# Loads of x in short pieces with six places, zeros moved behind the softmax, and a newly searched order

## The chip, the cores and the metric

The kernel runs on one core of one Trainium2 chip. The metric is the device time of one execution in microseconds (us); lower is better. Of several runs the median is given. A profile is one more execution, recorded by the hardware profiler; its span goes from the first to the last instruction of the program, and its own time lies a little over the span.

Five engines work side by side: TensorE (PE; its weight loads are shown as PEld), VectorE (DVE), ScalarE (ACT), GpSimd (POOL) and SyncE (SP). Each has its own stream of instructions, executed in order, and they wait for each other through semaphores. Data moves between HBM and the on-chip memory by DMA.

## The reference

Two layers follow each other. The first is a causal convolution of 7 taps, whose weights come from a softmax and differ by head (8 heads of 24 columns). The second mixes tokens; its matrix product over all tokens can be regrouped.

```python
# x: (8, 4224, 192), weight: (8, 7)
w = softmax(weight, axis=-1)
x_pad = concatenate([zeros((B, 6, D)), x], axis=1)
out[b, s, h*24+g] = sum_k w[h, k] * x_pad[b, s + k, h*24+g]

# y = out; w_q, w_k: (192, 64), w_out: (192, 192)
wq, wk = y @ w_q, y @ w_k
W_tok = scale * einsum('bsd,btd->bst', wq, wk)
mixed = einsum('bst,btd->bsd', W_tok, y)
return maximum(mixed, 0) @ w_out
```

## The kernel before

Everything on the chip is in bf16, except sums and the output. x of all 8 batches has room on the chip at once (`XW`), so no load of x ever waits for a buffer.

**Tiling.** A batch of 4224 tokens is cut into 35 chunks (`NCC`) of 122 tokens. A chunk is loaded as 128 rows, 6 of them from the chunk before, so that the convolution becomes one matrix product with a band matrix `BAND` for each head. Chunk 0 (122 rows and 6 rows of zeros) and chunk 34 (82 rows) have loads of their own. Chunks are worked on in groups (`groups_of`): four groups of up to 9 for batch 0, two groups (18 and 17) for each other batch.

**Loads.** `gen_load` makes the loads of one group: one DMA for all its full chunks, plus the small one at the batch's start or end. POOL issues them, converting f32 to bf16 on the way; they are all of POOL's work apart from the identity matrix (`ident`). All loads of a group count on one semaphore. The three weights come over SP, after the second group of batch 0 has landed.

**Start.** `WT_F` (the softmax input) is loaded by SP. DVE writes ones, several zeros and then, step by step, the softmax: `wmx` (L461), two subtractions (L467, L473), the sum, the reciprocal and the taps (L494); ACT does the exponential. PE spreads the taps over the diagonals (`spread`, L508) into two PSUM banks, and ACT and DVE copy one bank each into `BAND` (L527).

**Per batch**, for each group: `conv` on PE (four operations, each with two heads in halves: L391 and L392 through the helper `halves`) and its eviction to `Y` (L671, ACT or DVE). Then over chunks: the transposes `tr_lo` (L395, L396) and `tr_hi` (L726), evicted to `YTL` and `YTH` (L698, L733); the queries `wq` (L751, L755), evicted to `WQT`; the Gram matrix `gram` of Y (L787), summed in a bank of its own over the batch. From this a small matrix M is made (`turn`, `m`), and for each of five blocks of tokens `mix_lo` (L878) and `mix_hi` (L890) give the mixed tokens, evicted with relu to `RT` (L907, L908). `fin_hi` (L935) and `fin_lo` (L391, L392) multiply with `w_out`, the result is evicted to `OUT` (L970) and stored by SP (L978).

**Tile shapes of PE.** `mix_lo` and `fin_hi` use weights of 64 rows and 128 columns, everything else weights of 128 (or fewer) rows and 64 columns, in pairs. The planner counts a cost (`SWITCH`) where PE changes from one to the other.

**Order.** All operations are listed first, each with what it needs, a length and a due time. `Planner.plan` then puts them in an order, engine by engine, always the operation that can begin and whose due time is lowest. The due times are the numbers in `TURNS`, one for each operation, found beforehand by a search; `STAY` is added where PE would change the tile shape, `HOLD` is how long it may wait for an operation of the same shape. `op.lands` and `op.tail` tell the planner when a load is to be counted as landed. `Program.place` writes the streams and puts in a wait for each semaphore that an engine isn't yet known to have passed; a second and further wait is an instruction of its own (L269).

Of the kernel before, what the change touches and what calls it, by code (L numbers as in the profile page):

```python
# [13 lines left out]
    int(t) / 1000  # L14
    for t in """
-9360 -9860 -8870 -8880 -9260 -9760 -9760 -9160 -9060 -8960 -8910 -8910 -8860 -9360 -9310 -9360 -9360
-9300 -9290 -9280 -8360 -8260 -8210 -8360 -8160 -7960 -7910 -7860 -7360 -7260 -6960 -7260 -4360 -10360
-4260 -4160 -4060 -4040 -3360 -3260 -3160 -4360 -4360 -4360 -4360 -4360 -4360 -4360 -4360 -4360 -4360
-3360 -3340 -3260 -3240 -2360 -2340 -2260 -2240 -1360 -1340 -1260 -1240 -360 -340 -260 -240 640 660 740
760 1640 1660 1740 1760 2640 2660 2740 2760 -480 -5256 -3269 -5639 -2436 -6119 -4785 -6922 -2697 -6547  # L20
-2900 -8184 -3709 -11773 -2741 -3270 -6090 -11945 -3405 -6849 535 -5290 -3070 -5355 -2914 -5199 -4248
-3270 -5203 -8176 -5200 -3617 1049 7270 -1527 1452 -125 437 -1115 2575 669 4462 -4008 2241 -736 2188
-3392 2688 -366 4671 2314 4774 1510 -5859 -1080 1650 3655 -2805 -2225 2863 3712 -4982 -214 3624 -440
5811 168 -43 -4182 2328 1099 2977 4333 5544 2125 -4960 -5487 -5264 -3044 -1246 -5292 -632 -6217 -764
-74 -1078 1645 -1059 -604 310 -1847 1633 809 1261 1148 1774 613 1995 -221 2133 3240 -1868 3227 -220 725
-412 3895 1345 -3908 -437 2412 1145 -3912 1759 7529 -2401 -2511 -376 -45 -770 179 75 1157 1606 377 1178
2478 1419 2696 -2691 660 4785 4565 7183 -1945 323 1366 4118 -874 -955 202 -527 -342 -901 930 -907 356
2535 1985 1382 772 4127 1260 -1111 124 1160 1068 -949 2843 737 1947 1165 1141 1963 1865 1015 1391 1447
1702 -74 1049 2157 -573 -696 2171 3091 -3875 1621 1815 2057 1336 1560 3406 350 3930 1811 1631 806 1533
-2176 120 -160 307 697 392 -607 2158 1443 1095 4683 784 2578 2771 4703 2742 7357 3260 5899 3463 6217  # L30
3645 8560 -333 6048 2165 -3227 -299 4804 1442 -269 2464 1033 2330 -2282 2380 4417 716 -49 3007 5023
2635 1331 4441 4948 2995 6849 3538 5333 2785 2768 -3179 -2909 4430 6167 8185 2441 2170 3478 2909 2541
554 -2341 2444 1927 -821 1930 2471 1683 3865 3015 2812 1681 1913 2901 2236 -1040 2160 2775 2437 2022
2264 1982 2456 530 2945 -625 83 2391 2437 -247 4869 10274 3843 686 -2295 3278 468 -2877 2621 3234 3552
5619 5142 2314 3447 -712 2811 2566 3158 2537 2842 2785 -1373 2551 2194 3151 4852 2972 5013 3067 6779
3044 1235 3763 8267 3776 5123 4769 7025 4778 6514 4876 4862 2843 3189 4464 -186 3400 3287 1517 170 3082
4632 173 2822 4141 2345 4919 -1156 3870 4328 3579 2730 2456 3119 1411 4084 5177 4842 -327 4148 4784
2483 12403 11388 12726 1688 187 6372 10131 3246 4258 -1702 3458 4182 -118 2930 2729 1882 4669 8253 3861
3544 1615 3872 -172 2986 3160 3716 -1740 4531 9062 4005 3598 4951 3990 4363 2435 3391 -188 774 5121
6256 1049 3585 3961 4077 3890 4171 3621 2923 4666 7097 2748 2343 3820 2734 3811 2033 5780 3818 8021  # L40
2648 2954 4015 5571 3280 -1286 3326 1296 4205 -77 4486 1455 4875 3311 5075 4171 5445 4695 5467 3840
5547 6065 4545 4764 3889 874 4988 5384 3296 1407 5065 3706 4229 1167 4799 5495 -1008 2735 5015 4824
-216 1086 4797 3220 6247 4075 6903 8096 2585 2446 2397 3366 12419 11466 9645 4504 4002 2353 3004 4592
2447 1923 4855 3304 3544 3930 4268 4563 -31 1642 3776 4290 -862 3100 4826 6478 4160 4860 2445 3040 6705
3413 4148 6792 4180 4104 2785 4391 4686 4414 786 5937 2381 5714 4010 4678 4791 3602 4621 5486 -3702
4694 4691 4776 4745 8565 4811 2733 1579 4439 3726 3846 1552 3006 3416 5091 3731 3114 391 4950 -191 4947
1241 5561 6938 5922 7844 6076 5816 6857 5549 6431 8495 5919 4361 1180 965 5336 3713 5074 2853 2377 5685
3499 1703 6336 5580 6743 3976 5914 890 3735 -850 6119 5447 4947 4119 5702 6592 2952 2914 3851 5062
11027 10134 10283 4336 4832 2354 5585 5204 5235 5902 4279 5332 6811 4930 5452 70 7184 7777 5311 5310
3592 2752 3699 4914 5160 5093 886 6992 7265 5826 4610 2412 5386 6402 2677 5391 5863 3510 6078 4797 3048  # L50
3549 7308 4286 5112 2810 5621 5940 3872 3652 3847 6176 6516 2312 5811 4551 3444 5310 2800 3910 6703
2902 3118 6150 4601 5838 5604 6069 7926 5802 5058 6795 5408 6694 6497 7055 7466 7544 6117 8040 8562
2857 4878 6430 1709 6339 6247 4084 2149 3587 4651 7375 5911 5923 8233 4224 5104 7135 8548 7626 1422
6752 7520 5954 8811 9981 10001 3331 2861 1100 5523 5736 7942 8989 6855 6991 3418 3771 5267 6754 6792
5257 8583 2774 5930 5621 6098 8589 5981 7588 10163 5667 7262 8790 2009 6160 6573 7890 9275 9286 4367
8366 1994 4430 8376 2928 6391 6798 7671 9079 8471 6945 8447 929 3104 8245 1738 6621 7113 7765 8298
10610 7609 8976 2499 6811 5339 3124 4383 3701 4861 7650 5674 5118 6955 3022 7026 1967 7057 1554 7391
6867 7378 5794 8478 7540 10493 11198 10567 7886 9868 8667 7608 6132 7813 12143 8053 10500 4734 5726
10278 10809 6108 7660 6892 9279 8811 10480 9400 11789 6610 6051 11636 12987 12320 10573 10429 10064
11172 6766 7180 6653 8881 8940 8302 8163 3734 5115 8337 5917 10881 1732 6196 10991 548 6570 3947 6628  # L60
5684 11786 5374 8456 5972 5205 7358 2365 6800 7531 8553 12143 9541 7507 4239 2615 6653 8229 3661 7031
8556 8852 7269 9218 4711 5758 2449 5650 7927 7690 7261 10545 9140 8476 10487 4525 3241 2208 7451 8457
7788 6544 11624 6678 6638 3216 7890 3616 6282 3822 7930 5698 8782 6900 4062 5129 6641 6131 8120 8832
8094 4423 8160 8786 8210 8027 5877 5536 6062 1738 8351 8563 8713 4799 8391 5602 10941 9278 9705 9844
6685 7724 8581 9175 4769 3738 8621 7276 9572 10940 8347 11120 8993 5619 8811
# [38 lines left out]
class Planner:  # L104
# [6 lines left out]
    STAY = 0.865  # L111

    HOLD = 1
# [166 lines left out]
def bass_lightweight_conv__then__hypermixer_token_mlp_kernel(  # L280
# [43 lines left out]
    def semaphore(name):  # L324
        return es.enter_context(nc.semaphore(name))
# [48 lines left out]
    def bank(i, n=1):  # L374
        return PS[:, i * 512 : (i + n) * 512]
# [18 lines left out]
    def turn_halves(e, out, in_, identity):  # L394
# [34 lines left out]
        1250,  # L429
# [28 lines left out]
        200, needs=[ident], vt=-8.92)  # L458
# [44 lines left out]


    bands = []
    for q0, engine in ((0, "ACT"), (4, "DVE")):

        def spread(e, op, q0=q0):  # L508
            last = None
            for q in range(q0, q0 + 4):  # L510
                last = halves(
                    e,
                    bank(op.bank)[:, (q - q0) * 128 : (q - q0 + 1) * 128],
                    STEPT[0:112, 112 - 16 * q : 240 - 16 * q],
                    TAPS[0:112, :, :].rearrange("p i h -> p (i h)"),
                    start=q == q0,
                    stop=q == q0 + 3,
                    skip_group_check=True,
                )
            return last  # L520

        fill = add("PE", spread, 260, needs=[taps, stept], banks=1, vt=-7 + 0.1 * q0)

        def band(e, op, q0=q0, fill=fill):
            dst = BAND[:, :, 16 * q0 : 16 * q0 + 64]
            src = bank(fill.bank).rearrange("p (j h) -> p h j", h=H)
            return e.copy(dst, src) if op.engine == "ACT" else e.tensor_copy(dst, src)  # L527

        bands.append(add(engine, band, 550, drains=fill, vt=-6.9))
# [3 lines left out]
    at = [5000.0]  # L533

    def gen_load(b, gi):
        sem = semaphore(f"s_x{b}_{gi}")
# [4 lines left out]
        if cs[0] == 0:  # L541
            parts.append((XW[KC - 1 : 128, b, 0, :], bass.AP(x_t, base, [[D, CW], [1, D]])))
        n = len(full)
        parts.append(
            (
                XW[:, b, full[0] : full[0] + n, :],
                bass.AP(x_t, base + (CW * full[0] - KC + 1) * D, [[D, 128], [CW * D, n], [1, D]]),
            )
        )
# [9 lines left out]
        at[0] += len(cs) * 260.0  # L559
        load[b, gi] = []  # L560
        for k, part in enumerate(parts):
            first = (b, gi) == (0, 0) and part[0].shape[1] > 1 and len(part[0].shape) == 3
            op = add(
                "POOL",
                lambda e, op, part=part: e.dma_start(*part),  # L565
                900,
                needs=[zero_x] if cs[-1] == NCC - 1 else [],
                after=[] if first else [ident],
                dma=(f"x{b}_{gi}", sem, 16),
                vt=-10 if first else -4 + b + gi * 0.1 + 0.02 * k,  # L570
            )
            op.tail = 1500.0
            op.lands = at[0]
# [485 lines left out]
```

## Time and profile before

| what | us |
|---|---|
| median of 3 runs | 177.06 (177.01 to 177.64) |
| the profiled execution | 177.53 |
| its span | 175.7 |
| first `conv` matmul | 8.76 |
| second `conv` group of batch 0 | 11.62 |
| first `conv` of batch 1 | 23.53 |
| first `conv` of the last group | 133.97 |
| last store issued | 171.7 |

Mean granted clock of TensorE in this execution: 0.990.

Some landings of x, from issue to the moment when the whole load was there: the first load (8 chunks of batch 0) 1.30 to 6.46 us; the second group of batch 0 3.21 to 10.79; the last of batch 0 6.14 to 15.14; the 17 chunks of batch 1's first group 7.23 to 21.30; those of its second group 25.59 with the last; the first group of batch 2 30.25; the last load of all 52.46 to 106.0.

The page gives the DMA loads of the queues as a share of 16 engines' time. A share over 100% in a stretch means that one DMA engine had more than one packet under way.

```
q0 software_dynamic: 36128, 13.61, 65.1%      (x; POOL)
q1 hardware_dynamic: 12000, 26.31, 40.9%      (weights and out; SP)
q8 instruction: 25, 0.41, 0.9%
```

The columns are packets, MB and share. In lines of waits the columns are: who waited, for whom, us in total, times, longest. In a timeline they are: start, length, engine, line, operation, tiles and shapes, and in brackets the idle time of the engine before it. "issue" stands for a wait that no semaphore in the profile explains.

### The profile page before, as it was taken

The numbers are of one execution on the slowest core, as the hardware profiler recorded it, in microseconds if no ns is written. First come the engines' busy times: TensorE is split into PE (matmuls) and PEld (weight loads), VectorE is DVE, ScalarE is ACT, GpSimd is POOL, SyncE is SP. The second block draws the span as 40 slices with busy tenths as digits, with TensorE's granted clock in tenths as the row PEclk, the third lists the DMA queues.
The fourth block names the chain that finished last, engine by engine and source line by source line (L and its number), as shares of the span: only waits on it lengthen the run. The fifth ranks groups of instructions, "written<-read, shape, count | busy, mean of one in ns | idle before, by whom it ended". The sixth has DMA issues, their size and how long they took to land.

```text
span 175.7 us, 7099 instructions
## 1 busy us (share of the span) xinstructions
PE 157.1 (89%) x3226; PEld 121.7 (69%) x3226; DVE 118.0 (67%) x216; ACT 123.5 (70%) x206; POOL 30.3 (17%) x39
## 2 busy tenths in 40 slices
PE   0289799888999999899989979999999999999990
PEld 0179666776787787668778766878767777877550
DVE  6556587765766677586787738689688675765740
ACT  3243677597787948668648747888888896698980
POOL 7999452524230000000000000000000000000000
PEclk9999999999999999999999999999999999999995
DMA  3999999999999999999999999067283045987787
GB/s 30 162 189 186 205 191 193 191 196 277 193 279 194 286 309 268 343 250 243 304 264 282 237 194 348 24 244 297 103 343 127 4 175 216 356 347 309 265 303 262
DMA packets 48157, 40.36 MB, mean 230 GB/s; under 512 B 37632, under 2 KB 40960, under 8 KB 48128
## 3 DMA queue, kind: packets, MB, share of 16 engines
q0 software_dynamic: 36128, 13.61, 65.1%
q1 hardware_dynamic: 12000, 26.31, 40.9%
q8 instruction: 25, 0.41, 0.9%
q14 instruction: 4, 0.03, 0.1%
HBM read 27.56 MB, written 25.95 MB: 305 GB/s over the span
## 4 chain that ended last, share of the span: by engine, by line
PE 88%; issue 4%; DVE 3%; ACT 2%
PE ps L391 25%; PE ps L787 14%; PE ps L935 8%; PE ps L392 7%; PE ps L395 6%; PE ps L726 6%; PE ps L878 5%; PE ps L751 4%; PE ps L890 4%; PE ps L755 4%; PE ps L396 3%; ACT rt L907 1%; ACT out_sb L970 1%; DVE band L527 0%; DVE xw L416 0%
## 5 line engine op out<-in xcount | busy, mean ns | idle before, releaser
L970 ACT COPY out_sb<-ps 128x768 f32<-128x768 f32 (+1 forms) x46 | 34.7, 768 | 15.1 <-PE ps L392 11.3
L671 ACT CAST y<-ps 122x816 bf16<-122x816 f32 (+3 forms) x46 | 35.7, 791 | 13.2 <-PE ps L392 12.8
L907 ACT ACTIVATE rt<-ps 128x1024 bf16<-128x1024 f32 (+3 forms) x44 | 34.1, 800 | 6.4 <-PE ps L878 4.5
L787 PE MATMUL ps<-y 122*64 122x192 bf16 (+4 forms) x840 | 33.8, 222 | 2.2 <-issue 2.2
L970 DVE COPY out_sb<-ps 128x768 f32<-128x768 f32 (+1 forms) x26 | 21.6, 840 | 19.7 <-PE ps L392 18.5
L392 PE MATMUL ps<-wol,rt 128*64 128x192 bf16 x264 | 33.9, 255 | 1.0 <-issue 1.0
L787 PEld LDWEIGHTS ps<-y 122*64 122x64 bf16 (+1 forms) x840 | 31.1, 112 | 4.9 <-issue 2.8
L565 POOL DMA_DIRECT2D xw<-in_x_dram x34 | 29.9, 893 | 22.3 <-issue 21.5
L391 PE MATMUL ps<-wol,rt 128*64 128x192 bf16 x264 | 33.7, 255 | 0.0
L391 PE MATMUL ps<-xw,band 128*64 128x432 bf16 (+3 forms) x144 | 31.8, 335 | 1.5 <-DVE band L527 0.9
L392 PE MATMUL ps<-xw,band 128*64 128x432 bf16 (+3 forms) x144 | 32.1, 337 | 1.1 <-issue 1.1
L391 PEld LDWEIGHTS ps<-wol,rt 128*64 128x64 bf16 x264 | 24.1, 138 | 8.1 <-issue 2.0
L908 DVE TENSOR_SCALAR rt<-ps 128x512 bf16<-128x512 f32 (+3 forms) x36 | 23.6, 674 | 8.2 <-PE ps L878 7.6
L671 DVE CAST y<-ps 122x864 bf16<-122x864 f32 (+3 forms) x26 | 23.6, 912 | 8.0 <-PE ps L392 7.5
L698 DVE COPY ytl<-ps 128x976 bf16<-128x976 bf16 (+1 forms) x40 | 23.0, 591 | 3.9 <-PE ps L396 3.3
L392 PEld LDWEIGHTS ps<-wol,rt 128*64 128x64 bf16 x264 | 24.1, 138 | 1.2 <-issue 1.2
L396 PE MATMUL ps<-ident,y 122*64 122x122 bf16 x280 | 21.1, 219 | 0.0
L395 PE MATMUL ps<-ident,y 122*64 122x122 bf16 x280 | 21.0, 219 | 0.0
L935 PE MATMUL ps<-woh,rt 64*128 64x192 bf16 x264 | 20.4, 250 | 0.2 <-ACT rt L907 0.2
L395 PEld LDWEIGHTS ps<-ident,y 122*64 122x64 bf16 x280 | 18.1, 112 | 2.0 <-issue 0.5
L726 PE MATMUL ps<-ident,y 122*64 122x122 bf16 (+1 forms) x344 | 17.1, 220 | 1.3 <-DVE y L671 0.7
L396 PEld LDWEIGHTS ps<-ident,y 122*64 122x64 bf16 x280 | 17.7, 112 | 0.0
(95 smaller groups left out, 218.8 us busy)
## 6 DMA issues: line engine op xcount, KB each, us to landing
out_dram<-out_sb SPq DMA_DIRECT2D x28, 768.0 KB, 5.1
xw<-in_x_dram POOLq DMA_DIRECT2D x7, 816.0 KB, 33.2
xw<-in_x_dram POOLq DMA_DIRECT2D x7, 768.0 KB, 33.7
out_dram<-out_sb SPq DMA_DIRECT2D x8, 384.0 KB, 3.3
xw<-in_x_dram POOLq DMA_DIRECT2D x2, 432.0 KB, 8.3
out_dram<-out_sb SPq DMA_DIRECT2D x8, 96.0 KB, 4.3
xw<-in_x_dram POOLq DMA_DIRECT2D x1, 384.0 KB, 5.2
xw<-in_x_dram POOLq DMA_DIRECT2D x8, 45.8 KB, 25.0
```

The source lines that it names most:

```text
L391: e.matmul(out[0:64], lhsT[:, 0:64], rhs, **k)
L392: return e.matmul(out[64:128], lhsT[:, 64:128], rhs, **k)
L395: e.transpose(out[0:64], in_[:, 0:64], identity)
L396: return e.transpose(out[64:128], in_[:, 64:128], identity)
L565: lambda e, op, part=part: e.dma_start(*part),
L671: return e.copy(dst, src) if op.engine == "ACT" else e.tensor_copy(dst, src)
L726: last = e.transpose(ps[64 * i : 64 * i + HI, o : o + w], Y[0:w, yb, c, LO:D], IDENT[0:w, 0:w])
L787: mm = e.matmul(bank(GB)[p : p + 64, o : o + z - r], Y[0:w, yb, c, r : r + 64], Y[0:w, yb, c, r:z], start=st, stop=end, skip_group_check=True,
L907: return e.activation(dst, src(), AF.Relu)
L908: return e.tensor_scalar(dst, src(), 0.0, None, op0=ALU.max)
L935: last = e.matmul(bank(op.bank + a)[:, o : o + D], RT[64 * a : 64 * a + HI, slot, 2, i:n:nt], WOH[64 * a : 64 * a + HI, :], start=i == q, ...
L970: return e.copy(dst, src) if op.engine == "ACT" else e.tensor_copy(dst, src)
```

## The change

**Loads.** For batches 1 to 7 the full chunks of a group are loaded in pieces of two chunks (one piece of three in the group of 17), so a batch has 18 loads instead of 4. There are six semaphores, taken in turn. From the seventh on, a load waits on POOL until the load six before it, which had the same semaphore, has landed. Batch 0 is loaded as before, but with a semaphore for each load. A group's first `conv` waits for all semaphores that its loads counted on. The planner gets other figures for loads (issue, `tail`, `lands`).

**Zeros.** The memsets of `WQT`, `WQH`, `YTH`, `WKT`, `WKB` and `MBD` on DVE come after `taps`, the last step of the softmax.

**Band.** It is spread into four PSUM banks instead of two, in pieces of 32 columns a head, which ACT and DVE copy in turn.

**Order.** `TURNS`, `STAY` and `HOLD` are new, and the planner's length of `ident`.

```diff
@@ TURNS, STAY, HOLD
-    int(t) / 1000
+    int(t) / 1e6
...
-    STAY = 0.865
-
-    HOLD = 1
+    STAY = 1.104146
+
+    HOLD = 2.100438
@@ ident, own: the planner's length and due time
-        1250,
+        700,
...
@@ zeros
+    for zero in (zero_w, zero_q, zero_yt, *zero_k, zero_m):
+        zero.after.append(taps)
@@ band
-    for q0, engine in ((0, "ACT"), (4, "DVE")):
+    for q0, engine in ((0, "ACT"), (2, "DVE"), (4, "ACT"), (6, "DVE")):
...
-            for q in range(q0, q0 + 4):
+            for q in range(q0, q0 + 2):
...
-            dst = BAND[:, :, 16 * q0 : 16 * q0 + 64]
-            src = bank(fill.bank).rearrange("p (j h) -> p h j", h=H)
+            dst = BAND[:, :, 16 * q0 : 16 * q0 + 32]
+            src = bank(fill.bank)[:, 0 : 32 * H].rearrange("p (j h) -> p h j", h=H)
@@ gen_load
-    at = [5000.0]
+    NLOAD = 6
+    S_LOAD = [semaphore(f"s_x{i}") for i in range(NLOAD)]
+    small_loads = []
+    LANDS = [6000.0, 9900.0, 12300.0, 13900.0]
...
-        n = len(full)
-        parts.append(
-            (
-                XW[:, b, full[0] : full[0] + n, :],
-                bass.AP(x_t, base + (CW * full[0] - KC + 1) * D, [[D, 128], [CW * D, n], [1, D]]),
+        pieces = len(full) // 2 if b else 1
+        for k in range(pieces):
+            some = full[len(full) * k // pieces : len(full) * (k + 1) // pieces]
+            parts.append(
+                (
+                    XW[:, b, some[0] : some[0] + len(some), :],
+                    bass.AP(x_t, base + (CW * some[0] - KC + 1) * D, [[D, 128], [CW * D, len(some)], [1, D]]),
+                )
             )
...
+            slot = len(small_loads) % NLOAD
+            gate = small_loads[-NLOAD:][:1] if b and len(small_loads) >= NLOAD else []
             op = add(
                 "POOL",
                 lambda e, op, part=part: e.dma_start(*part),
-                900,
-                needs=[zero_x] if cs[-1] == NCC - 1 else [],
-                after=[] if first else [ident],
-                dma=(f"x{b}_{gi}", sem, 16),
+                610 if b else 900,
+                needs=[*([zero_x] if cs[-1] == NCC - 1 else []), *gate],
+                after=small_loads[-1:] if b else [] if first else [ident],
+                dma=(f"x_{slot}", S_LOAD[slot], 16) if b else (f"x0_{gi}_{k}", semaphore(f"s_x0_{gi}_{k}"), 16),
...
-            op.tail = 1500.0
-            op.lands = at[0]
+            op.tail = 4200.0 if b else 1500.0
+            op.lands = 0.0 if b else LANDS[gi]
+            if b:
+                small_loads.append(op)
```

## The prediction, made before the result was known

> **What bounds the kernel now.** I read the first two parts of the page first, then sums by stretch of time, then TensorE's own waits, then the DMA view.
>
> ```profile
> PE 157.1 (89%) x3226; PEld 121.7 (69%) x3226; DVE 118.0 (67%) x216; ACT 123.5 (70%) x206; POOL 30.3 (17%) x39
> PE   0289799888999999899989979999999999999990
> DMA  3999999999999999999999999067283045987787
> ```
>
> TensorE (PE) sets the end. DVE and ACT have a third of their time free. PE's row has dents in its first 60%, none after that; DMA is full over the same 60%. The table by stretch (PE, PEld, DVE, ACT, POOL busy, clock, DMA share, GB/s) says the same in microseconds:
>
> ```profile
> 16.00:106.00 90.00, 84.59 (x1834) 66.99 (x1828) 62.58 (x108) 63.93 (x111) 15.49 (x18) 1.00 1.40 245
> 106.00:170.00 64.00, 63.80 (x1265) 47.15 (x1263) 46.00 (x79) 53.87 (x86) 0.00 (x0) 1.00 0.59 227
> ```
>
> From 16 to 106 us PE is idle for 5.41 us, from 106 to 170 us for 0.20. The granted clock is 1.00 in both. 106 us is when the last x has landed: its load was issued at 52.46 us and landed 53.5 later. What PE waits for (us in total, times, longest):
>
> ```profile
> PE ps L395 <- DVE step L435: 3.6, 1, 3.6
> PE ps L391 <- DVE taps L494: 2.9, 1, 2.9
> PE ps L787 <- issue: 2.2, 2, 1.3
> PE ps L392 <- issue: 2.1, 2, 1.1
> PE ps L391 <- DVE band L527: 0.9, 1, 0.9
> PE ps L726 <- DVE y L671: 0.7, 1, 0.7
> PE ps L391 <- issue: 0.6, 1, 0.6
> PE ps L726 <- issue: 0.5, 1, 0.5
> ```
>
> The waits for DVE all lie before 11.2 us: the softmax and the band matrix. The "issue" waits are the 5.41 us: 1.28 at 19.20 us, 0.08 at 26.86, 0.50 at 32.64, 1.07 at 39.08, 0.90 at 70.06, 0.59 at 89.60, 0.99 at 102.10. No semaphore explains them; one is in the middle of one `fin_lo`:
>
> ```profile
> 101.85 0.25 PE L391 MATMUL ps<-wol,rt 128*64 128x192 bf16 x1
> 103.09 0.30 PE L392 MATMUL ps<-wol,rt 128*64 128x192 bf16 x1 [0.99 <-issue]
> ```
>
> The DMA view of 100.7 to 102 us shows what went before it:
>
> ```profile
> q8 instruction: 1, 0.02, 4.6%
> ```
>
> Each of the six long waits has such a packet shortly before it: it starts at 18.01, 30.78, 37.69, 68.66, 87.76 and 100.72 us, takes 0.95, and PE goes on 1.35 to 1.5 us after its end. All 25 are 16 KB. So PE's instructions arrive by DMA, and PE runs dry when one is late. The packets before 101 us follow each other by 6.0 to 6.9 us (13 intervals), the first one with x nearly done by 3.8 (100.72, 104.50): x in the rings costs such a fetch up to some 2.5 us. After 106 us none is late enough to stall PE, though stores of out go on.
>
> **The change part by part**, against the profiled execution (span 175.7, time 177.53, so 1.8 outside the span; it is 0.47 over the median of 177.06).
>
> *Loads in pieces.* Batches 1 to 7 get 126 loads for 28, almost all of two chunks: 256 packets, 16 for each of 16 DMA engines, where a load of 17 chunks puts 136 on each. At most six stand in the rings; before, POOL put in what the rings would take (it waited seven times for "issue", 21.5 us). The trace has no fetch behind short loads, so bounds: nothing gained (0), or all seven stalls gone (-5.4). If a fetch comes 0.63 us earlier (a quarter of the 2.5), 0.65 + 0.44 + 0.27 + 0.36 = 1.7 us of stalls stay; at 1.25 us earlier 0.03. I take 1.4 us left, since loads that are held back also last longer and meet more fetches: **-4.0**.
>
> The Trainium skill (DMA: Bandwidth & Descriptors, "Queues, rings and completion order") says that each DMA engine goes round its queue rows and drains one packet, typically 9 to 17 descriptors and at most 64, before it changes rows. By that rule it does not matter how many loads are queued behind the first, and a limit of six alone gains nothing; only shorter packets would. The trace is on its side in one point: the stall at 19.20 us, with loads that took 14 us to land, is no shorter than that at 102.10 us, with loads that took 53.
>
> *The gate.* Each of these loads waits on POOL for the one six before it. Behind it on POOL are only later loads, and behind those the `conv` of their group. A load of 2 chunks should cost POOL 0.55 (the 122-row load) + 134/2054 of the way to 1.28 (17 chunks): 0.60 us. Round trip, by the nearest rows: 2.9 us (`wt_f`, 28 KB) at least, 5.2 (the first load, 8 chunks on empty rings) at most; over six, 0.48 to 0.87 us a piece, with POOL's 0.60 as the floor. Before, these 126 pieces' worth landed from 15.1 to 106.0 us: 0.72 each. What the new order can stand: I counted the matmuls ahead of each group's first `conv` in the built program, took when that many had begun in the trace, less the stalls until then, and set it against the old landing. Batch 1: matmul 273, 22.56 - 1.28 = 21.28 against 21.3, slack 0.0; its second half (408) 28.26 against 25.6, slack 2.7. Batch 2 (626) 38.55 against 30.25, 8.3; last group (2510) 128.3 against 106.0, 22.3. So only batch 1 is near its load. Bounds 0 to +1.5; I take **+0.5**.
>
> *Semaphores.* A group's first `conv` waits for six instead of one. In the built programs PE has 80 semaphore instructions for 48; the trace's take 51 ns each. 32 x 51 ns = 1.6 if all are exposed, 0 if matmuls of 408 columns cover them (they do in mid-stream, where PE shows no gap around one). I take **+0.3**.
>
> *Zeros behind the softmax; band in four.* The six memsets take 0.40 us (3.02 to 3.42, ahead of `step`) and 0.42 (4.28 to 4.70, ahead of `wmx`, whose weights landed at 3.75). `taps` ends 0.8 earlier, at 5.9. Then they run while DVE would wait for PE (1.16 us idle before L527), but end near 6.8, after the first fill. Two casts of 256 columns on each of DVE and ACT, at some 0.40 (0.69 and 0.58 for 512), end near 7.6: first `conv` at 7.75 instead of 8.76, -1.0. The x for it landed at 6.77. But `gram` now stands right behind the second `conv` group and waits for its eviction, as L726 waits 0.70 now, with nothing between: +0.7. Together **-0.3** (bounds -1.0 to +0.2).
>
> *Order.* The same 3226 matmuls. Tile shape changes between 64-row and 128-row weights 98 times for 106. Such a step (L935 to L391, 101.46 to 101.63) takes 0.17 us, a step inside `fin_lo` 0.08: 8 x 0.1 = **-0.8** (bounds -1.2 to 0; new waits for an eviction up to +1.5, which DVE and ACT at 70% make unlikely).
>
> Sum: -4.0 + 0.5 + 0.3 - 0.3 - 0.8 = -4.3. Span 171.4, time 172.8 set against the median.
>
> **Rivals.** (a) *Forecast, fetches come in time*: 172.8, 0.58. (b) *The fetch wait is fixed, stalls stay*: a fetch waits for what one engine already has in hand, six pieces or sixty. For it: the stalls do not grow with the backlog. Against: they end with the last x, and pieces put 16, not 136, packets on an engine at once. Then the sum is -0.3: 176.8, 0.15. (The rule of the Trainium skill above would give this, if it is the number of loads that matters.) (c) *Batch 1 comes late*: its slack is 0.0, and its seventh to ninth piece wait for a landing near 15.4 us. Two more microseconds at that `conv`: 174.8, 0.11. (d) *The gate throttles x*: if a round trip stays above 6 x 0.90 = 5.4 us, the last group misses 128.3 us ((128.3 - 15.1) / 126 = 0.90). At 5.7 us (0.95 a piece) it lands at 134.8, 6.5 late, against the 4.3 gained: 179.3. For it: landings of 5.2 us alone, up to 33 behind others, and the stores share the engines from 36 us. Against: 0.72 with full rings. 0.13. (e) *New waits for evictions* of 3 us: 175.8, 0.03.
>
> **How the numbers follow.** The time is (a)'s. Its own range, all stalls gone and the best order to few gone, is 170.3 to 174.9. (b), (c) and (e) carry it to 177.3; (d) is left out above. Within 0.5% (0.9 us, about what a measurement of this kernel can tell from no change) lies most of (b) beside the first half microsecond of (d). Faster: (a), (c), (e) and a third of (b), 0.77. Same 0.08. Slower, the rest of (d) and a little of (b), 0.15.
>
> **What would show it.** In the new profile: PE's "issue" waits before the last x lands fall from 5.4 to about 1.4 us, and 16 KB instruction packets keep their number; if they stay with shorter loads, (b). No wait of the first `conv` of a group for x beyond batch 1; if there are, (d), and POOL's landings are over 5.4 us. First `conv` near 7.75 us, and a new gap near 12 to 14 us. Wrong altogether, if PE waits for evictions in mid-stream, where it now has none.

## The result, and the profile after

The changed kernel takes 187.22 us (median of 4, 186.91 to 188.49), the kernel before 177.35 beside it: a ratio of 1.056, 95% interval 1.049 to 1.063. It is slower by 10 us; 172.8 was forecast, with 177.3 as the upper end of the range. Medians are of all runs; ratios leave out runs over 1.5% above the fastest of the same kernel (some of e3 to e8 and e11), and the profiles of e3, e4, e6 and e7, taken in such runs, are read for the kind of a wait more than its size.

The first lines of the new page, then its chain that ended last:

```profile
PE 160.2 (86%) x3226; PEld 124.0 (67%) x3226; DVE 120.1 (65%) x214; ACT 122.7 (66%) x210; POOL 94.1 (51%) x137
...
PE   0588999999987399979998739999999999999970
...
POOL 7936899979354869476854779816400000000000
PEclk9999999999999669999999978999999999999995
...
DMA 39%; PE 37%; POOL 17%; issue 3%; DVE 1%; ACTq 0%; ACT 0%; POOLq 0%
DMA xw<-in_x_dram 39%; POOL xw L617 17%; PE ps L432 11%; PE ps L989 5%; PE ps L841 4%; PE ps L932 3%; PE ps L433 2%; PE ps L436 2%; PE ps L944 2%; PE ps L780 2%; PE ps L805 2%; PE ps L809 1%; PE ps L437 1%; DVE out_sb L1024 1%; DVE rt L962 0%
```

PE's row has two holes that were not there, at the 14th and the 24th slice; there and in the slice right behind, the row of the granted clock falls. The chain, which was PE's before, now goes back through the loads of x and POOL, which issues them. (Line numbers have moved: the convs, once L391 and L392 with `xw`, are L432 and L433.) What PE waits for:

```profile
PE ps L432 <- DMA xw<-in_x_dram: 9.5, 3, 4.2
PE ps L436 <- DVE step L476: 3.3, 1, 3.3
PE ps L432 <- DVE taps L535: 2.6, 1, 2.6
PE ps L432 <- ACT out_sb L1024: 1.1, 1, 1.1
PE ps L432 <- issue: 0.8, 2, 0.6
PE ps L841 <- DVE y L725: 0.7, 1, 0.7
```

The waits for "issue" have fallen from 5.4 to 0.8 us (0.9 with those too short for this list), as forecast. In their place stand three waits for x: 1.12 us at 50.82, 4.17 at 59.20, 4.25 at 105.64. The sums by stretch show what follows the two long ones (columns as before; the clock is the last figure but two):

```profile
16.00:61.65 45.65, 41.86 (x953) 33.45 (x949) 32.37 (x56) 31.40 (x62) 34.55 (x51) 1.00 1.20 192
61.65:68.47 6.82, 5.10 (x40) 3.29 (x42) 2.17 (x3) 2.01 (x3) 4.58 (x7) 0.50 1.17 156
68.47:109.43 40.96, 35.40 (x746) 27.22 (x742) 26.46 (x46) 28.31 (x43) 28.08 (x41) 1.00 1.23 232
109.43:112.85 3.42, 2.96 (x34) 2.63 (x36) 1.18 (x2) 1.37 (x4) 3.38 (x6) 0.50 1.28 140
112.85:139.00 26.15, 26.13 (x560) 20.68 (x557) 17.56 (x28) 20.94 (x35) 12.48 (x18) 1.00 1.12 241
```

For 10.24 us the clock is granted at half; PE is busy for 8.06 of them (5.10 + 2.96), and in the rest it still stands still. Single matmuls show it too: two following convs of one group start 0.18 us apart at full clock (51.93 and 52.11) and 0.31 apart at 63.37 and 63.69, where they are a little shorter (408 columns for 432).

Why x is late, by the DMA issues from 36 to 120 us (KB of each, us from issue to landing):

```profile
xw<-in_x_dram POOLq DMA_DIRECT2D x70, 96.0 KB, 5.4
```

A load takes 5.4 us here in the median, 11.1 at most. The last x lands at 138.3 us instead of 106.0: 0.985 us for each of the 126 loads after batch 0's last at 14.2.

### The profile page after: what moved, and what is told of

It reads as the page before. It is cut to its first block, busy times and chain, and to the rows that moved or that the text cites. A ratio compares the mean times of both kernels' runs of the same rounds, so it can differ in the third digit from the quotient of the medians.

```text
span 185.6 us, 7231 instructions
## 1 busy us (share of the span) xinstructions
PE 160.2 (86%) x3226; PEld 124.0 (67%) x3226; DVE 120.1 (65%) x214; ACT 122.7 (66%) x210; POOL 94.1 (51%) x137
## 4 chain that ended last, share of the span: by engine, by line
DMA 39%; PE 37%; POOL 17%; issue 3%; DVE 1%; ACTq 0%; ACT 0%; POOLq 0%
DMA xw<-in_x_dram 39%; POOL xw L617 17%; PE ps L432 11%; PE ps L989 5%; PE ps L841 4%; PE ps L932 3%; PE ps L433 2%; PE ps L436 2%; PE ps L944 2%; PE ps L780 2%; PE ps L805 2%; PE ps L809 1%; PE ps L437 1%; DVE out_sb L1024 1%; DVE rt L962 0%
## 5 line engine op out<-in xcount | busy, mean ns | idle before, releaser
L617 POOL DMA_DIRECT2D xw<-in_x_dram x132 | 93.7, 719 | 39.9 <-DMA xw<-in_x_dram 31.7
L725 ACT CAST y<-ps 122x816 bf16<-122x816 f32 (+3 forms) x42 | 31.8, 785 | 21.5 <-PE ps L433 21.1
L432 PE MATMUL ps<-xw,band 128*64 128x432 bf16 (+3 forms) x144 | 33.5, 355 | 11.5 <-DMA xw<-in_x_dram 9.5
L725 DVE CAST y<-ps 122x864 bf16<-122x864 f32 (+3 forms) x30 | 27.7, 930 | 22.3 <-PE ps L433 22.0
L841 PE MATMUL ps<-y 122*64 122x64 bf16 (+2 forms) x840 | 34.0, 223 | 0.7 <-DVE y L725 0.7
L433 PE MATMUL ps<-xw,band 128*64 128x432 bf16 (+3 forms) x144 | 33.6, 357 | 0.0
L432 PE MATMUL ps<-wol,rt 128*64 128x192 bf16 x264 | 32.9, 253 | 0.6 <-issue 0.6
L841 PEld LDWEIGHTS ps<-y 122*64 122x64 bf16 x840 | 30.8, 113 | 3.4 <-DVE y L725 1.0
L433 PE MATMUL ps<-wol,rt 128*64 128x192 bf16 x264 | 32.8, 253 | 0.0
L432 PEld LDWEIGHTS ps<-wol,rt 128*64 128x64 bf16 x264 | 23.8, 138 | 6.3 <-issue 1.3
L432 PEld LDWEIGHTS ps<-xw,band 128*64 128x64 bf16 x144 | 14.8, 121 | 17.3 <-issue 13.4
L1024 DVE COPY out_sb<-ps 128x768 f32<-128x768 f32 (+1 forms) x20 | 18.5, 925 | 10.3 <-PE ps L433 9.3
L433 PEld LDWEIGHTS ps<-wol,rt 128*64 128x64 bf16 x264 | 23.9, 138 | 0.7 <-issue 0.7
L436 PEld LDWEIGHTS ps<-ident,y 122*64 122x64 bf16 x280 | 18.2, 112 | 2.9 <-DVE y L725 1.1
L825 ACT CAST wqt<-ps 128x512 bf16<-128x512 f32 (+1 forms) x22 | 11.7, 542 | 9.7 <-PE ps L809 7.5
```

The source lines that it names most:

```text
L432: e.matmul(out[0:64], lhsT[:, 0:64], rhs, **k)
L433: return e.matmul(out[64:128], lhsT[:, 64:128], rhs, **k)
L436: e.transpose(out[0:64], in_[:, 0:64], identity)
L841: mm = e.matmul(bank(GB)[p : p + 64, o : o + z - r], Y[0:w, yb, c, r : r + 64], Y[0:w, yb, c, r:z], start=st, stop=end, skip_group_check=True,
```

## The experiments

In all but e4 and e10, which start from the kernel before, the order of every engine is the one of the changed kernel, as the planner had it; e1 to e3, e5 to e8 and e11 rewrite only the loads, e9 adds matmuls, and e12 rewrites the loads and moves a few operations. Waits are from one profiled execution each, times from several.

### Without the gate (e1)

```diff
+    for (b, gi), ops in load.items():
+        if b:
+            one_for_all = semaphore(f"s_g{b}_{gi}")
+            for op in ops:
+                k = small_loads.index(op)
+                if k >= NLOAD:
+                    op.needs.remove(small_loads[k - NLOAD])
+                op.dma = (f"g{b}_{gi}", one_for_all, 16)
```

> The changed kernel with the order of every engine as it is and all its short loads, but without the gate: one semaphore for each group, no load waits for another. Theory 1 (the limit of six is what makes x late; the changed kernel waited 9.5 us for x in three places and ran 10.2 us at half clock after two of them): no wait of PE for x over 0.5 us, clock 0.99, about 187.2 - 9.5 - 5.1 = 172.6 us if instruction fetches stay as they are in the changed kernel (0.9 us of waits for 'issue'), about 177 if they come late again because the rings are full. Theory 2 (the short loads themselves are too slow, 126 of them at 0.72 us on POOL): x still lands at 0.9 us a load or slower, waits of 4 us or more stay, over 182 us. Theory 3 (the new order asks too early): over 182 us as well.

177.79 us, ratio to the kernel before 1.0005 (0.996 to 1.005). PE's waits after the start:

```profile
PE ps L841 <- issue: 1.7, 3, 0.8
PE ps L437 <- issue: 0.8, 2, 0.6
PE ps L841 <- DVE y L725: 0.7, 1, 0.7
PE ps L436 <- DVE y L725: 0.7, 1, 0.7
PE ps L780 <- issue: 0.7, 1, 0.7
```

No wait for x, and the clock stays at 1.00. So the limit of six (with the six semaphores that belong to it), not the short loads, cost 9.4 of the 10 us. But the waits for "issue" are back at 3.5 us: short loads alone don't keep the fetches in time.

### The old loads in the new order (e2)

One load for a group's full chunks again, no gate: the loads as before the change, the rest as changed.

> The changed kernel with every engine's order as it is, but the loads of batches 1 to 7 as before the change: one of 17 or 16 chunks for a group, no gate. Theory 1 (the limit) and theory 2 (short loads): no wait for x beyond batch 1, clock 0.99; the stalls for 'issue' are back at 4 to 6 us before the last x has landed; 176 to 177.5 us, since start and tile changes gain 1 us. Theory 3 (the order): over 180 us. Against e1 it tells whether short loads without a limit keep the instruction fetches in time: e1 3 to 4 us under e2 if the length of a load decides, the same if the number under way decides.

176.28 us, ratio 0.995 (0.989 to 1.001). PE waits 3.1 us for "issue" and once for x of batch 1:

```profile
PE ps L432 <- issue: 1.3, 1, 1.3
PE ps L432 <- DMA xw<-in_x_dram: 1.2, 1, 1.2
```

The new order and start are no worse than the old, perhaps 1 us better (the interval reaches from -1.9 to +0.2 us). Between e1 and e2 the waits for "issue" are the same within what single profiles scatter, so the length of a load doesn't decide them. e1 is 1.5 us over e2 for another reason, told in the last section.

### The new loads in the old order (e4)

The kernel before, each of its loads replaced by its pieces, with six places.

> The kernel before, with its order, start and due times, and the new loads alone: pieces of two chunks, six places. Theory 1: x lands as late as in the changed kernel (last load near 138 us, pace 0.98 us a load); the old order asks for batch 2 earlier (34.4 us for its first conv, 36.9 there; 37.8 for its second half, 44 there) and for batch 3 too (47.7 against 52), so PE waits for x already in batch 2, 8 us or more in total; 185 to 192 us. Theory 3 (the order): 175 to 178 us.

190.93 us, ratio 1.054 (1.048 to 1.061), runs from 186.7 to 194.1. In the profile:

```profile
PE ps L391 <- DMA xw<-in_x_dram: 11.9, 3, 4.2
PE ps L391 <- issue: 2.8, 1, 2.8
PE ps L787 <- issue: 1.2, 2, 0.7
```

The same waits for x without the new order, so theory 3 falls. e2 and e4 together are the change cut in two: the order about -1 us, the loads some +10. But here the same short loads with the same six places leave 4.0 us of waits for "issue", one of them 2.76 us long at 26.95 us: six places alone don't bring the fetches in time.

### Twelve, eight and seven places (e3, e5, e6)

```diff
+    PLACES = 12
+    S_MORE = [*S_LOAD, *[semaphore(f"s_y{i}") for i in range(PLACES - NLOAD)]]
+    for k, op in enumerate(small_loads):
+        if k >= NLOAD:
+            op.needs.remove(small_loads[k - NLOAD])
+        if k >= PLACES:
+            op.needs.append(small_loads[k - PLACES])
+        op.dma = (f"x_{k % PLACES}", S_MORE[k % PLACES], 16)
```

> The changed kernel with its order as it is and twelve places instead of six (a load waits for the one twelve before it). Theory 1: twelve places let a load take 10.8 us from issue to landing before x is late (12 x 0.90), so POOL's 0.72 us a load sets the pace; no wait for x over 0.5 us, clock 0.99, 172.5 to 174 us. Theory 2: as the changed kernel, over 182 us.

> The changed kernel, order as it is, eight places instead of six. Theory 1 (the limit sets the pace: 0.985 us a load with six, so 6/8 of it, 0.74, which is POOL's own pace): no wait for x over 0.5 us and no half clock in mid-kernel. The waits for 'issue' should lie between those with six places (1.0 us in all) and with twelve or no limit (7.6 and 3.5): about 2. Together 174.5 to 177 us. If instead the DMA engines are what x waits for, the round trip grows with the places, and PE still waits for x by 4 us or more: over 180.

> As before with seven places. Theory 1: 0.985 x 6/7 = 0.84 us a load, just under the 0.90 that the order can stand: waits for x under 1.5 us in all, waits for 'issue' 1 to 2, 174 to 177 us. If a store's burst rather than the mean pace decides, single waits of 2 to 4 us stay, each with half a clock window or more behind it: 178 to 184.

| places | us | ratio | last x lands | us a load | times places | PE waits for x | for "issue" |
|---|---|---|---|---|---|---|---|
| 6 (changed) | 187.22 | 1.056 (1.049 to 1.063) | 138.3 | 0.985 | 5.9 | 9.5 | 0.9 |
| 7 (e6) | 186.33 | unclear | 133.2 | 0.94 | 6.6 | 8.6 | 2.6 |
| 8 (e5) | 178.31 | 0.996 (0.991 to 1.000) | 127.5 | 0.90 | 7.2 | 0.9 | 2.8 |
| 12 (e3) | 179.12 | 1.007 (1.002 to 1.012) | 112.7 | 0.78 | 9.4 | 0 | 7.6 |
| no limit (e1) | 177.79 | 1.000 (0.996 to 1.005) | 115.9 | 0.81 | | 0 | 3.5 |

"Us a load" counts from 14.2 us in every row; "times places" is the round trip, that is, how long a place is taken by one load. With six, seven and eight places it is close to 2.3 + 0.6 x places (5.9, 6.5, 7.1): it grows with the places, so loads that are under way together slow each other. With six, 0.985 is over the 0.90 that the order can stand; with eight it is just that, and one wait of 0.9 us is left. The row of twelve lies on the same line (9.5), but it is no evidence for it: there POOL waits for a place for 7.8 us in all (31.7 with six), and its own 0.76 us for an issue makes most of the 0.78. Without any limit x is no faster.

The expectations of e3, e5 and e6 failed: the round trip grows with the places, so eight gave 0.90, not 0.74, and seven is still late. With twelve the waits for "issue" came back so strongly that nothing was won. e5's runs spread from 175.7 to 181.3, e6's from 182.0 to 187.8. At the edge of the pace it may be chance how stores and loads meet; what differs between these runs was not looked at.

### Four chunks a load (e7, e8)

Two neighbouring pieces are issued as one, with six and four places.

> The changed kernel, order as it is, pieces of four chunks and six places: as many chunks under way as with twelve places of two, in half as many loads. If what a late instruction fetch stands behind is counted in chunks, the waits for 'issue' are those of twelve places or of no limit (3.5 to 7.6 us), 176.5 to 179 us; if it is counted in loads, they are those of six (1.0 us), and since x comes in time, 173 to 175 us.

> As the last with four places: sixteen chunks under way as in the run with eight places of two, in half as many loads, and POOL issues 10 loads a batch for 18. Same time as with eight places within 1 us if chunks under way decide; waits for x of 4 us and more if the number of loads under way decides the pace (four instead of six).

e7: 177.65 us, ratio 0.992 (0.987 to 0.996), runs from 174.9 to 181.8; PE waits 1.3 us for x and 5.1 for "issue". e8: 187.63 us, ratio 1.053 (1.046 to 1.061); 9.8 us for x, 3.0 for "issue". By the line above, a load of twice the size and four places gives 2.3 + 4 x 1.2 = 7.1 us; its 70 loads from 14.2 to 138.0 us took 1.77 x 4 = 7.1. So sixteen chunks under way don't give the same pace whatever their cut: the number of loads decides, as the second reading had it. The line is only a rough one, though: for six places of the double size it gives 9.5 us, and e7 took 1.47 x 6 = 8.8; for six short loads it gives 5.9, and e4 took 6.4.

For "issue" no count orders all profiles. Six places of two chunks gave 0.9 us in the changed kernel but 4.0 in e4, seven 2.6; sixteen chunks under way gave 2.8 and 3.0 (eight loads or four), 24 gave 7.6 and 5.1 (twelve or six); and no limit at all gave 3.5 (e1), 3.1 (e2) and 5.4 (before). How late a fetch comes for how much under way is therefore not shown.

### PE kept busy while it waits (e9)

```diff
+    FILL = 18
...
+    def filler(e, op):
+        for _ in range(FILL):
+            halves(
...
+    for op in planner.order:
+        if getattr(op, "place", None) in ((3, 1, 0), (6, 0, 0)):
+            op.filler = filler
```

> The changed kernel with 18 pairs of matmuls of 512 columns (3.8 us at full clock) in front of the wait for x in the two places where PE stood still for 4.2 us (first conv of batch 3's second group, first conv of batch 6). They write the bank that this conv overwrites. x comes no earlier. If the half clock follows from PE standing still, it stays at 1.00 there and 10.2 us at half clock, 5.1 us of work, are won: 181 to 183 us. If the clock falls for another reason, or half clock costs nothing since PE would wait anyway, 186 to 188 us.

186.48 us, ratio 1.050 (1.047 to 1.054). The stretch of the first filler, then the one in which PE stood still next, and the one after:

```profile
59.60:63.40 3.80, 3.80 (x46) 2.05 (x42) 1.33 (x3) 0.19 (x1) 3.75 (x6) 1.00 1.05 253
...
78.00:81.10 3.10, 0.00 (x0) 0.00 (x0) 0.38 (x2) 0.28 (x1) 1.34 (x2) 1.00 1.33 244
81.10:84.50 3.40, 3.25 (x20) 1.94 (x22) 0.80 (x2) 1.63 (x2) 3.33 (x5) 0.50 1.27 259
```

Both halves of the expectation were needed. The clock does follow from PE standing still: with the filler it stays at 1.00 there and in the other place. But PE then comes earlier to a conv whose x has not landed, stands still for 3.28 us and pays the half clock there. About 1 us is won at most, since x sets the pace: most of the time that the half clock takes would otherwise have been a wait for x.

### x of two batches only (e10)

> The kernel before, without the loads of x of batches 2 to 7: their convs read the x of batch 1, so batches 2 to 7 of the output are computed from batch 1. Everything else is as before. If x in the rings is what makes instruction fetches late, the waits for 'issue' from 26 us on (4.1 us in the profile before) are gone, and the time is near 177.5 - 4.1 = 173.4 us. If stores or the fetches' own distance make them late, 2 us or more of these waits stay: 175.5 to 177.

171.45 us, ratio 0.963 (0.961 to 0.965). By stretch:

```profile
26.00:106.00 80.00, 80.00 (x1733) 63.70 (x1730) 60.59 (x104) 62.00 (x100) 0.00 (x0) 1.00 0.37 144
```

After the last x at 25.7 us PE is never idle in mid-kernel; one wait for "issue" is left, 1.7 us at 18.80, while x is still coming. Stores go on as before. So x under way makes the fetches late. The gain is 6.0 us by the two profiled spans (6.6 by the medians), more than the 4.1 us of gaps. The two traces have the same 3226 matmuls in the same order, so they can be compared one by one. From 26 us on the kernel before falls back by 6.0 us in nine steps, each 127 matmuls or a multiple of that (to within one) after the last; the 25 packets of 16 KB for 3226 matmuls come about as often. Six of the steps are the waits for "issue", each some 0.2 us more than its gap (5.5 us for 4.1); the other three, 0.16 to 0.20 us each, show no gap. So the rest of the gain goes to the same fetches, and a gap for "issue" understates its price.

### Looking for a version under both (e11, e12)

e11 has short, limited loads for batch 1 alone; e12 is e2 with two moves by hand on PE, one out of the wait of 0.7 us for an eviction, one out of that for x of batch 1.

> The changed kernel, order as it is, with short loads and six places for batch 1 alone; from batch 2 on the long loads as before the change, without a gate. In the changed kernel there was no wait for x and 0.2 us for 'issue' until 36 us; with long loads there were 3.1 us for 'issue' and 1.2 for x of batch 1. If both hold here, waits are 1.8 us (the late part of those for 'issue') to 3: 174.5 to 176 us, under both kernels and under the one with long loads throughout (176.3). If x of batch 2, issued from 24 us on instead of 8, comes late for 36.8 us, a wait and a half-clock window cost 3 to 5 us: 178 to 181.

> The kernel of e2 (order, start and band of the changed kernel, loads as before the change) with two moves by hand on PE: the gram that waits 0.7 us for an eviction at 14 us goes behind the first two convs of batch 0's third group, whose x has landed by then, and the first two convs of batch 1, which waited 1.2 us for x, go behind the next four operations. If both waits vanish without others in their place: 176.3 - 1.9 = 174.4 us, 1.5 to 2% under the kernel before. If x of batch 1 is simply not there earlier, the second wait comes back at the next step: 175.6. No gain: 176.3.

e11: 178.78 us, ratio 1.003 (1.000 to 1.006); no wait for x, 2.9 us for "issue", nothing won. e12: 177.04 us, ratio 0.996 (0.993 to 0.998). The gap at 14 us is gone, but 0.8 us for an eviction stand at 23.42 and 0.2 at 21.34 instead, and the waits for "issue" are 3.4 us, so of the 1.9 us nothing is seen beyond e2. e2 and e12 are 0.4 to 0.5% under the kernel before (for e2 the interval includes no change); that is all these runs found among kernels that load all of x.

## Why the prediction was wrong

**The step that failed is the gate.** It was put at +0.5 us, with bounds 0 to +1.5, because the round trip lay, by the nearest rows, between 2.9 and 5.2 us. Both rows were loads without stores beside them. Measured: 5.9 us for a place's round trip, 5.4 in the median from issue to landing between 36 and 120 us, 11.1 at most; with the limit taken out (e1) the time falls by 9.4 us, although the waits for "issue" rise by 2.6 again, so by an estimate from these two the term was some 12 us. The point from which it decides was worked out rightly (5.4 us, or 0.90 a load); the bounds were drawn so that they ended just under it.

What the bounds left out is in the trace of the changed kernel. The short loads issued from 16 to 36 us, before the first store, land in 3.9 us in the median and 4.9 at most. Of those issued later, the 12 that meet hardly any store (under 0.3 us) between issue and landing take 3.5 us in the median, the 80 others 5.9. So the bounds held as long as no store was under way. (This is a comparison inside one trace; no run takes the stores away.) The rows to look at were there: stores took up to 10.0 us to land in the kernel before, and between 57 and 77 us its 35 chunks of x took 20 us with full rings, 1.1 us for what is now a piece.

Rival (d) was the right one, with 0.13. Its price was too low: with the measured pace its own formula gives 15.1 + 126 x 0.985 - 128.3 = 10.9 us late, not 6.5, and so 183.7 us. The prediction also left out that PE's clock falls to half when PE stands still for 4 us, though that could not be seen in the profile of before, which has no such wait in mid-kernel. e9 shows that this adds little of its own as long as x sets the pace.

**POOL's issue** was put at 0.60 us a load by drawing a line between 122 and 2176 rows; it took 0.72 to 0.77. Before the stores begin this alone sets the pace, at 139 GB/s for 194 in the same stretch before the change (POOL is the fifth pair, with 18.15 of 20 us):

```profile
16.00:36.00 20.00, 19.83 (x497) 16.93 (x495) 15.64 (x29) 14.08 (x33) 18.15 (x27) 1.00 1.24 139
```

**The fetches.** The waits fell from 5.4 to 0.9 us, with 1.4 forecast to be left, and e10 shows that x under way is the cause. That the six places did it is not shown: in e4 they left 4.0 us in the old order. Some luck is in the size, then. Rival (b) was half right: that loads are short does nothing by itself (3.5 us in e1 for 3.1 in e2). By the rule of the Trainium skill (DMA: Bandwidth & Descriptors, "Queues, rings and completion order") the number queued would not matter. The runs don't settle it: 0.9, 2.8 and 7.6 us at six, eight and twelve places speak against it, 4.0 in e4 and 3.5 without a limit for it, one profile each.

**Start and order.** First conv at 7.93 us, 7.75 forecast; the gap behind the second group came as worked out, 0.70 us at 14.11. e2 puts start and order together at -0.9 us by its ratio, with an interval that includes 0; the two terms sum to -1.1. Rival (c) was not seen in the changed kernel: PE had no wait for x at batch 1 (0.2 us for "issue" at 20.79), while the long loads of e2 had 1.2. No wait was seen for the 32 further semaphore instructions either.

Together, by PE's gaps: 9.5 for x, 4.0 lost at half clock (half of the 8.06 us that PE was busy there), 1.1 for an eviction at 80.32, less 4.5 for "issue" and 0.8 for the start: +9.3, and the span grew by 9.9. The 5.1 us for the half clock in the expectations of e1 and e9 count the waits for x inside these stretches once more. (This says where the time lies, not what the removal of one item alone would win.)

## What to carry to other kernels

A limit on transfers under way sets a pace, round trip over places, as long as the issuing engine isn't slower still. Take the round trip from the busiest stretch, with everything else that moves there, and compare it with the latest moment that each consumer can stand; where a range for it ends close under the deciding value, the other side deserves more than a small chance. When a price depends on two sides (here x against instruction fetches), look for a limit that serves both before trusting either: here none of those tried did, and leaving the loads alone was as good.

## What was not expected of the hardware

A pause of 2.2 us can be enough for half clock. In e3 PE did 0.41 us of work in 2.57 us, and the next 3.41 us ran at half:

```profile
19.00:21.57 2.57, 0.41 (x17) 0.26 (x12) 0.00 (x0) 1.85 (x9) 1.71 (x3) 1.00 1.55 194
21.57:24.98 3.41, 3.41 (x55) 2.82 (x51) 2.47 (x6) 0.00 (x0) 3.28 (x5) 0.50 1.58 188
```

In e4 a pause of 2.76 us did the same. In e6 one of 2.43 us at 68.30 did not, nor one of 2.42 us at 68.36 in e8, nor any under 2 us; every one of 3.2 us or more did. All half-clock stretches in mid-kernel last 3.41 us or twice that. An estimate from these rows: if the clock is decided in windows of that length, they fit: counted back from e6's own fall at 107.46 us and e8's at 106.64 in steps of 3.41, a boundary lies near 69.9 and 69.1 us, inside each pause, while the pauses of e3 and e4 lie whole in the window that ends with the fall. The Trainium skill (TensorE: Matmul & The Clock Gate, "What's actually happening") tells of a free-running window of 3413 ns. That agrees with these rows. The Trainium skill (TensorE: Matmul & The Clock Gate, "Why this matters for your kernels") also advises against gaps over about 3 us. By these rows that is too generous.

Starts differ too, and the same window may be why. In the changed kernel the convs of batch 0's third group start 0.10 us apart at 15.3 us, in e1 0.18 us apart at 15.9. The first record of full clock is at 13.86 us in one and at 19.21 in the other; the page's row shows 9 in both. It costs about 2 us, and e9 and e11 had it as well. In the two profiles e1 is 2.2 us behind e2 at the 200th matmul; e2 then waits for x of batch 1, and with the differing waits for "issue" 1.5 us are left at the end. Whether it is so in all their runs was not looked at.

What stays open is where in the DMA engines an instruction fetch waits, since no record tells when it was asked for.
